# Decayed linear attention beside an FFN on one core: products and state of a token tile called in one piece

## The chip, the cores and the metric

One core of one Trainium2 chip runs the whole program. The metric is the device time of one execution in microseconds (us), and 854.63 us is the median of three runs. A profile of one further execution says what each engine did when: TensorE (PE, with its weight loads shown apart as PEld), VectorE (DVE), ScalarE (ACT), GpSimd (POOL) and SyncE (SP), which issues most transfers.

## The reference

Three stages follow each other. The first is a decayed linear attention with a bonus for the present token, over 4 sequences, 8 heads, 768 tokens and 48 numbers per head:

```python
for t in range(S):
    kt, vt, rt = (k[:, :, t], v[:, :, t], r[:, :, t])
    cur = np.einsum('bhd,bhe->bhde', u[None] * kt, vt)
    y[:, :, t] = np.einsum('bhd,bhde->bhe', rt, state + cur)
    state = w[None, :, :, None] * state + np.einsum('bhd,bhe->bhde', kt, vt)
```

The second is an FFN on all 3072 tokens of 384 numbers, with 2048 inner columns: `h = x @ w_in`, `g = h - tanh(h)`, `x = g @ w_out`. The third sends each token to the one of 8 experts that fits best (a normalised product with 8 embeddings), and puts it through that expert's two matrices (384 by 1024 and back) with a relu between, times the gate.

## The kernel before, in words

The 3072 tokens stand in 24 tiles of 128 (`n`), and three tiles make a block (`TB = 3`, eight blocks `j`). Tile `n` is chunk `n // 4` of sequence `n % 4`, so that the state a tile needs was left by the tile four places earlier.

Attention of one tile is an object `Att`. It is computed by chunk: `scores` (line 361) multiplies decayed keys `KT` with decayed queries `RT` into the PSUM tiles `pa`, two heads at a time on the two halves of the array; `causal` (line 366, DVE) copies the strictly causal part of `pa` over `am`, in which `diagonal` (line 350) had put the bonus of each token on the diagonal; `values` (line 391) multiplies `am` with the values and, for chunks after the first, `RT` with the old state, into the PSUM tile `py`, with outputs of 32 columns on the four quarters of the array side by side. `result` copies `py` into the block's operand `xt` as two halves, high and low, for the FFN (lines 396 and 397). `state` multiplies decayed keys with values (line 405, PSUM tile `pst`) and adds to the state (line 414). `values(part, of)` can run a part of its list of products. The list is ordered so that products with the old state come first.

The FFN takes one step `i` per 128 inner columns. `ffn1` (line 470) makes nine matmuls of 384 columns into a PSUM tile `ph`; `squares` and `small_tanh` turn it, on ACT and DVE, into `ghi` and `glo` (the last of these by line 533 on DVE); `ffn2` (line 481) makes nine matmuls into three accumulators, three steps later (`LAG = 3`).

In the main loop, from the block with `j = 0` on, an FFN step of block `j` is called, and then as many pieces of the attention of a later block as are due: `attn_tile` is a generator, a piece is what stands between two `yield`s, and a tile has six. Blocks 3 to 7 are due 18 pieces in 12 steps, so one and two pieces by turns, and a tile takes four steps. Block 2 is due 18 pieces in 8 steps. In each step `ffn1`, the pieces, then `ffn2` are called. The routing of the block before (`finish`) is also spread over the steps, and contains small DVE instructions such as line 610. At the first piece of a tile, the SP queue is given the two loads of the next one (`load_rkv`, lines 304 and 305).

The order of calls isn't yet the order on the engines. A planner goes through all instructions with a model of their times, takes those called earlier first, and takes later ones where the earlier aren't ready or have no buffer; what it makes is a fixed order for every engine. PSUM has eight tiles for all uses (`bufs=8`).

Of the kernel before, what the change touches and what calls it, by code (L numbers as in the profile page):

```python
# [29 lines left out]
def rwkv__then__tanh_ffn__then__top1_moe_kernel(  # L30
# [22 lines left out]
    HP = H // 2  # L53
# [372 lines left out]
    def attn_tile(n, xt):  # L426
        t = Att(n, xt)
        t.decay_r(nc.vector)
        t.decay_k(nc.gpsimd)
        t.bonus(nc.gpsimd)  # L430
        t.sums()
        t.diagonal()
        t.decayed()
        yield
        t.scores((0, 1))
        yield
        t.scores((2, 3))
        t.causal()
        yield
        t.values(0, 2)  # L440
        yield
        t.values(1, 2)
        t.result()
        yield
        t.state()
        yield

    xts = {}
# [8 lines left out]
    def attention(j):  # L457
        xts[j] = work.tile([P, NK, 2, TOK], F32R, name="xt")
        for n in range(TB * j, TB * j + TB):
            if 2 * TB + 1 < n + 1 < NTILE:  # L460
                load_rkv(n + 1)
            yield from attn_tile(n, xts[j])
# [915 lines left out]
```

## Time and profile before

| what | value |
|---|---|
| median of three runs | 854.63 us (853.89 to 856.8) |
| profiled execution | 856.98 us, of which 855.4 us are span from the first to the last instruction |
| PE busy | 791.2 us, 92% |
| DVE busy | 532.5 us, 62% |
| ACT busy | 442.9 us, 52% |
| POOL busy | 308.9 us, 36% |
| mean granted TensorE clock | 0.956 of full speed |

The page gives busy time by engine; the share of the span isn't the share of a stage. Matmuls overlap, so the start of one to the start of the next says more than the length of one. In the timeline, instructions of one kind that follow each other are merged (`x9`), with the start of the first and the time to the end of the last; what stands in brackets is idle time ahead of them and the engine that ended it.

### The profile page before, as it was taken

The numbers are of one execution on the slowest core, as the hardware profiler recorded it, in microseconds if no ns is written. First come the engines' busy times: TensorE is split into PE (matmuls) and PEld (weight loads), VectorE is DVE, ScalarE is ACT, GpSimd is POOL, SyncE is SP. The second block draws the span as 40 slices with busy tenths as digits, with TensorE's granted clock in tenths as the row PEclk, the third lists the DMA queues.
The fourth block names the chain that finished last, engine by engine and source line by source line (L and its number), as shares of the span: only waits on it lengthen the run. The fifth ranks groups of instructions, "written<-read, shape, count | busy, mean of one in ns | idle before, by whom it ended". The sixth has DMA issues, their size and how long they took to land. (4 is left out here: it accounts for less than half of the span.)

```text
span 855.4 us, 15321 instructions
## 1 busy us (share of the span) xinstructions
PE 791.2 (92%) x5835; PEld 726.7 (85%) x5835; DVE 532.5 (62%) x1048; ACT 442.9 (52%) x1007; POOL 308.9 (36%) x312
## 2 busy tenths in 40 slices
PE   6567969999999999999999999999979999999992
PEld 3456969888989989979989989999869999999992
DVE  8999697566775765665675574576553434544520
ACT  1156646645555656645745645778343434444421
POOL 6673352057461371353173070051243034321211
PEclk7579989999999999999999999999989999999996
DMA  8742612035213213213123021041354255545400
GB/s 292 266 147 65 242 56 75 1 82 160 82 53 109 81 54 108 81 53 108 42 93 109 20 63 57 29 117 60 102 187 128 75 168 167 166 141 171 128 27 29
DMA packets 41446, 89.69 MB, mean 105 GB/s; under 512 B 9328, under 2 KB 21024, under 8 KB 40338
## 3 DMA queue, kind: packets, MB, share of 16 engines
q1 hardware_dynamic: 37042, 79.10, 28.4%
q0 software_dynamic: 4320, 9.51, 3.5%
q8 instruction: 48, 0.79, 0.4%
q14 instruction: 36, 0.29, 0.1%
HBM read 69.82 MB, written 19.47 MB: 104 GB/s over the span
## 5 line engine op out<-in xcount | busy, mean ns | idle before, releaser
L470 PE MATMUL ph<-xt,wq 128*128 128x384 f32 (+2 forms) x1712 | 345.7, 344 | 3.0 <-DVE am L366 2.6
L470 PEld LDWEIGHTS ph<-xt,wq 128*128 128x128 f32 x1712 | 306.2, 191 | 9.1 <-DVE am L366 2.7
L481 PE MATMUL acc<-wq,ghi 128*128 128x392 f32 (+2 forms) x1120 | 296.5, 348 | 2.6 <-DVE wq L286 1.9
L481 PEld LDWEIGHTS acc<-wq,ghi 128*128 128x128 f32 (+1 forms) x1120 | 201.5, 188 | 14.0 <-issue 7.1
L481 PE MATMUL acc<-wq,glo 128*128 128x392 f32 (+2 forms) x560 | 187.6, 343 | 5.8 <-DVE glo L533 5.8
L517 ACT ACTIVATE z<-ph 128x384 f32<-128x384 f32 x128 | 62.4, 488 | 110.9 <-PE ph L470 110.6
L526 DVE TENSOR_TENSOR ph<-ph,z 128x384 f32<-128x384 f32 x128 | 71.9, 562 | 69.5 <-ACT z L517 69.1
L481 PEld LDWEIGHTS acc<-wq,glo 128*128 128x128 f32 (+1 forms) x560 | 104.9, 188 | 8.2 <-DVE glo L533 6.1
L533 DVE TENSOR_TENSOR glo<-ph,ghi 128x384 fp32r<-128x384 f32 x128 | 70.8, 553 | 35.8 <-ACT ghi L528 35.2
L528 ACT ACTIVATE ghi<-ph 128x384 fp32r<-128x384 f32 x128 | 62.6, 489 | 46.4 <-DVE ph L527 41.7
L702 POOL DMA_INDIRECT out_dram<-ob,gts x27 | 28.7, 1061 | 155.6 <-ACT ob L780 150.1
L518 ACT ACTIVATE q<-z,sb_t 128x384 f32<-128x384 f32 x128 | 78.9, 616 | 3.4
L527 DVE SCALAR_TENSOR_TENSOR ph<-q,ph 128x384 f32<-128x384 f32 x128 | 71.8, 561 | 13.6 <-ACT q L518 4.3
L547 DVE SCALAR_TENSOR_TENSOR glo<-ph,ghi 128x384 fp32r<-128x384 f32 (+2 forms) x56 | 31.5, 563 | 74.5 <-ACT ghi L546 63.5
L530 ACT ACTIVATE mk<-z,lz_t 128x384 bf16<-128x384 f32 x128 | 77.0, 602 | 0.0
L749 DVE TENSOR_TENSOR wq<-eraw,wq 128x768 fp32r<-128x768 f32 x60 | 55.4, 961 | 17.9 <-ACT wq L748 16.3
L546 ACT ACTIVATE ghi<-ph 128x384 fp32r<-128x384 f32 (+2 forms) x56 | 27.7, 496 | 72.7 <-PE ph L470 70.7
L748 ACT ACTIVATE wq<-eraw 128x768 fp32r<-128x768 f32 x64 | 50.5, 837 | 12.5 <-DMA eraw<-in_moe_w_dram 12.5
L335 POOL TENSOR_TENSOR rk<-rkv 128x384 f32<-128x384 f32 x21 | 22.0, 1049 | 92.4 <-DMA xs<-xr 88.8
L350 POOL TENSOR_TENSOR am<-ident,cd 128x512 f32<-128x512 f32 x42 | 45.0, 1094 | 14.4 <-DVE cd L340 14.4
L391 PE MATMUL py<-am,rkv 128*32 128x128 f32 x704 | 42.0, 295 | 7.7 <-DVE am L366 4.1
L327 POOL TENSOR_TENSOR tt<-tt,tab_k 112x512 f32<-112x512 f32 x20 | 36.7, 1835 | 29.5 <-DMA tt<-in_cols_dram 27.7
(272 smaller groups left out, 898.6 us busy)
## 6 DMA issues: line engine op xcount, KB each, us to landing
eraw<-in_moe_w_dram SPq DMA_DIRECT2D x32, 768.0 KB
rkv<-in_rows_dram SPq DMA_DIRECT2D x22, 640.0 KB
tt<-in_cols_dram SPq DMA_DIRECT2D x22, 448.0 KB
xd<-xt SPq DMA_DIRECT2D x8, 1152.0 KB
wraw<-in_moe_w_in_dram SPq DMA_DIRECT2D x8, 768.0 KB
wraw<-in_moe_w_out_dram SPq DMA_DIRECT2D x8, 768.0 KB
xs<-xr SPq DMA_DIRECT2D x21, 192.0 KB
first<-in_rows_dram SPq DMA_DIRECT2D x1, 640.0 KB
```

The costliest lines, as they stand in the source:

```text
L350: nc.gpsimd.tensor_tensor(out=a, in0=ident[:, None, :].to_broadcast([P, HP, P]), in1=self.cd[:, :, g:g + 1].to_broadcast([P, HP, P]), op=A ...
L470: nc.tensor.matmul(out=ph, lhsT=lhs[a][:, kk, :], rhs=rhs(b, kk), start=(kk == 0 and p == 0), stop=(kk == nk - 1 and p == 2))
L481: mm = nc.tensor.matmul(out=acc[t], lhsT=g[a][:, t * P:t * P + m], rhs=rhs(b, i), start=(i == span[0] and p == 0), stop=(i == span[1] - 1 ...
L517: nc.scalar.activation(out=z, in_=ph, func=AF.Square)
L518: nc.scalar.activation(out=q, in_=z, func=AF.Square, scale=SS, bias=sb_t)
L526: nc.vector.tensor_tensor(out=ph, in0=ph, in1=z, op=ALU.mult)
L527: nc.vector.scalar_tensor_tensor(out=ph, in0=q, scalar=KC, in1=ph, op0=ALU.add, op1=ALU.mult)
L528: nc.scalar.activation(out=ghi, in_=ph, func=AF.Copy)
L530: nc.scalar.activation(out=mk, in_=z, func=AF.Relu, bias=lz_t, accum_out=zx[:, step:step + 1])
L533: nc.vector.tensor_tensor(out=glo, in0=ph, in1=ghi.bitcast(F32), op=ALU.subtract)
L748: nc.scalar.activation(out=hi[c][:, a], in_=t[:, a], func=AF.Copy)
L749: engs[s % len(engs)].tensor_tensor(out=lo[c][:, a], in0=t[:, a], in1=hi[c][:, a].bitcast(F32), op=ALU.subtract)
```

## The change

`attn_tile` calls the same instructions in other pieces. Before, scores were called in two pieces, the products in two and the state in one. Now all scores and the causal copy are one piece, two pieces are empty, and all products, the state and the result are one piece, with the state's calls ahead of the result's. A tile still has six pieces.

```diff
@@ -432,17 +432,16 @@
         t.diagonal()
         t.decayed()
         yield
-        t.scores((0, 1))
-        yield
-        t.scores((2, 3))
+        t.scores(range(HP))
         t.causal()
         yield
-        t.values(0, 2)
         yield
-        t.values(1, 2)
+        yield
+
+        t.values()
+        t.state()
         t.result()
         yield
-        t.state()
         yield
```

## Rows read from the trace of the kernel before

**Rows 1.** The page, busy us, share and instructions of PE and others.

```profile
PE 791.2 (92%) x5835; PEld 726.7 (85%) x5835; DVE 532.5 (62%) x1048; ACT 442.9 (52%) x1007; POOL 308.9 (36%) x312
```

**Rows 2.** Windows: length, then busy us by engine, granted clock, DMA share, GB/s.

```profile
core 0: us, PE busy (x) PEld busy (x) DVE busy (x) ACT busy (x) POOL busy (x), PEclk, DMA share, GB/s
...
210.00:528.00 318.00, 313.07 (x2674) 283.02 (x2673) 206.82 (x433) 184.96 (x447) 124.68 (x123) 0.99 0.23 75
528.00:856.00 328.00, 305.73 (x1742) 297.09 (x1741) 154.44 (x335) 153.11 (x308) 79.02 (x75) 0.97 0.35 114
```

**Rows 3.** Groups of PE's matmuls by line, from 210 to 528 us.

```profile
L470 PE MATMUL ph<-xt,wq 128*128 128x384 f32 x684 | 132.5, 337 | 0.0
L481 PE MATMUL acc<-wq,ghi 128*128 128x392 f32 x460 | 127.9, 355 | 0.0
L481 PE MATMUL acc<-wq,glo 128*128 128x392 f32 x229 | 79.0, 345 | 0.0
L391 PE MATMUL py<-am,rkv 128*32 128x128 f32 x480 | 27.8, 280 | 4.4 <-issue 1.8 <-DVE am L366 1.3 <-DVE ph L527 1.2
L391 PE MATMUL py<-tt,st 112*32 112x128 f32 x360 | 27.7, 281 | 0.5 <-DVE glo L533 0.5
...
L590 PE MATMUL pk<-oh,ones 128*128 128x8 bf16 x30 | 1.6, 166 | 0.0
```

**Rows 4.** Timeline of PE, a step without attention: start us, us, instruction.

```profile
335.20 1.73 PE L470 MATMUL ph<-xt,wq 128*128 128x384 f32 x9
...
338.37 1.75 PE L470 MATMUL ph<-xt,wq 128*128 128x384 f32 x9
```

**Rows 5.** Timeline of PE, one tile: scores, first half, second half with state.

```profile
344.74 1.74 PE L470 MATMUL ph<-xt,wq 128*128 128x384 f32 x9
...
349.20 1.73 PE L470 MATMUL ph<-xt,wq 128*128 128x384 f32 x9
350.86 0.42 PE L391 MATMUL py<-tt,st 112*32 112x128 f32 x8
351.22 0.44 PE L481 MATMUL acc<-wq,ghi 128*128 128x392 f32 x1
...
353.71 1.75 PE L470 MATMUL ph<-xt,wq 128*128 128x384 f32 x9
355.39 0.30 PE L391 MATMUL py<-am,rkv 128*32 128x128 f32 x1
...
356.40 0.56 PE L405 MATMUL pst<-rkv,ktok 128*48 128x48 f32 x16
356.90 0.62 PE L481 MATMUL acc<-wq,ghi 128*128 128x392 f32 x2
```

**Rows 6.** Timeline of PE, a tile with its first half in three parts.

```profile
387.61 1.73 PE L470 MATMUL ph<-xt,wq 128*128 128x384 f32 x9
...
392.64 1.73 PE L470 MATMUL ph<-xt,wq 128*128 128x384 f32 x9
...
397.51 1.73 PE L470 MATMUL ph<-xt,wq 128*128 128x384 f32 x9
```

**Rows 7.** Timeline of PE, a tile whose first half is late.

```profile
366.62 1.81 PE L470 MATMUL ph<-xt,wq 128*128 128x384 f32 x9
...
370.98 0.41 PE L391 MATMUL py<-am,rkv 128*32 128x128 f32 x4 [1.25 <-DVE ph L527]
...
375.07 1.20 PE L470 MATMUL ph<-xt,wq 128*128 128x384 f32 x6
```

**Rows 8.** Timeline of DVE ahead of that half: a long instruction, the causal copies.

```profile
361.74 3.68 DVE L610 TENSOR_SCALAR rn<-rn 128x3 f32<-128x3 f32 x1
...
370.20 1.34 DVE L366 COPY_PREDICATED am<-cmask,pa 128x512 f32<-128x512 uint8 x2
```

**Rows 9.** Timeline, all engines: the next tile's columns are loaded, decayed, used.

```profile
309.03 0.34 SPq L304 DMA_DIRECT2D tt<-in_cols_dram  x1
...
313.13 1.80 POOL L327 TENSOR_TENSOR tt<-tt,tab_k 112x512 f32<-112x512 f32 x1 [1.59 <-DMA tt<-in_cols_dram]
...
316.14 1.16 PE L361 MATMUL pa<-tt 48*128 48x128 f32 x16
```

## The prediction

> **What bounds the kernel now.** I read the busy times first: TensorE (PE) is busy for 791.2 us, 92% of the span [rows 1]. Then the stretches: attention of the third to eighth token block runs beside the first FFN and ends at 528 us, and from 210 us (the start of the fourth block's) to there PE is busy for 313 of 318 us while VectorE (DVE) is busy for 207 and ScalarE (ACT) for 185; after 528 us, where no attention runs, PE is still busy for 306 of 328 us [rows 2]. So in the stretch that the change touches nothing but PE's own queue sets the pace, and what follows is PE work again, which starts earlier by what is saved here. The question is therefore how many PE microseconds each form of the attention costs.
>
> The timeline of PE answers that with a ruler. An FFN step is 9 matmuls of line 470 and 9 of line 481. Between two starts of line 470 a step without attention takes 338.37 - 335.20 = 3.17 us [rows 4], 0.176 us for a matmul. Whatever a step takes above that is attention. A tile of blocks 3 to 7 goes through four such steps (18 pieces in 12 steps): preparation, scores, first half of the products, second half with the state.
>
> - Scores: 349.20 - 344.74 = 4.46 us, so 1.29 us extra. They already run in one piece, both quarters in the same step.
> - First half: 353.71 - 349.20 = 4.51 us, 1.34 us extra, for 24 of the 56 matmul instructions of the products (480 + 360 over 15 tiles [rows 3]; each fp32 matmul is two instructions). The planner sent the 8 that read only the old state at 350.86, one FFN matmul at 351.22, the other 16 behind it [rows 5].
> - In five of the 15 tiles the half is cut into three: 392.64 - 387.61 = 5.03 us, 1.86 us extra [rows 6].
> - Second half with the state: 397.51 - 392.64 = 4.87 us, 1.70 us extra [rows 6]. Without the state (last chunk, 4 tiles) it is 0.50 us less, as the state's row takes 356.90 - 356.40 [rows 5]: 1.20 us.
> - The half that is late, in three of the 15 tiles: 375.07 - 366.62 = 8.45 us. PE stands still until 370.98, because the masked scores `am` aren't written [rows 7].
>
> **The change, part by part.** *What is removed.* In blocks 3 to 7 (15 tiles) the step of the first half becomes a plain step of 3.17 us. I take its cost today from the whole stretch, so that late ones count as they were: 684 + 460 + 229 = 1373 FFN matmuls in 318.0 us [rows 2, 3] at 0.1761 us are 241.8 us; 76.2 us are left. The routing's small matmuls take about 2.4 us of that (an estimate: 45 of them at the 1.6 us / 30 of the largest group [rows 3]). Scores: 15 x 1.29 = 19.4 us. Second halves: 11 x 1.70 + 4 x 1.20 = 23.5 us. That leaves 30.9 us for the first halves, 2.06 us each against 1.34 us for an undisturbed one; some 8 us of it are lateness like that of [rows 7], whose tile alone lost 8.45 - 4.51 = 3.9 us.
>
> *What is added.* The 24 instructions join the run of the second half. A run of 8 takes 351.22 - 350.86 = 0.36 us, a run of 32 takes 356.40 - 355.39 = 1.01 us [rows 5], so 24 more inside a run cost 0.65 us: 15 x 0.65 = 9.8 us. No instruction is added or dropped. What vanishes is the cost of entering and leaving: 0.36 us plus the slower matmul on either side, against 0.22 us for the same 8 inside a run.
>
> *Difference for blocks 3 to 7*: 30.9 - 9.8 = 21.1 us less on PE.
>
> *Block 2* (three tiles, before 210 us) has 18 pieces in 8 steps, and there the old and new products of the second and third tile are called in the same step; I count nothing for them. Its first tile had its first half a step early as above: 1.86 - 0.65 = 1.2 us, by the cut form.
>
> *The waits that move.* Products start one FFN step later than before, so `am` gets 3.17 us more. In the late tile `am` was complete at 370.20 + 1.34 = 371.54 us; the new run would start at 366.62 + 3.17 + 1.58 = 371.37 us, and its first 0.36 us needs no `am` [rows 7, 8]. So the lateness fits, with 0.2 us to spare. What was late there is DVE, held for 3.68 us by an instruction on 3 elements a partition [rows 8], one of three such holds, one ahead of each late half; the change doesn't move them. I take 0.5 us as not hidden in each of the three worst tiles: -1.5 us. Both ends for the range: nothing paid, or all 8 us paid as now.
>
> The Trainium skill, "SBUF — State Buffer", section "SBUF: two separate sides", says that DVE and GpSimd share one pair of ports as an exclusive lock, so that one of them can stand still for a whole instruction of the other. The trace shows the hold of 3.68 us [rows 8] and agrees with the rule, but doesn't name the holder. By that rule the hold would come back unchanged beside the same GpSimd work, and if PE paid it in full the sum would be the one of the lateness rival below.
>
> *State and result.* The state's matmuls are called before the result's copy, but PE already ran them right behind the products, and the copy waits for the products alone. The copy comes 0.65 us later in its step; the block's operand is read four FFN steps (12.7 us) later, which hides it. Two DVE additions of the state come before the result's subtraction, as they already did. No DMA is moved, but the SyncE queue loads the next tile's columns when the products end: issue at 309.03, decayed keys ready at 313.13 + 1.80 = 314.93, scores on PE at 316.14 [rows 9], 1.2 us spare. The products' end and the next scores both move by 0.65 us within that loop, so the spare time stays; if it were gone, PE would wait in order with all FFN matmuls behind it. PSUM: the products' bank is taken a step later, which frees one bank for that step; the new run needs no more banks at once than the old second half.
>
> *Sum*: 21.1 + 1.2 - 1.5 = 20.8 us. The profiled execution took 856.98 us, 855.4 of it span; 856.98 - 20.8 = 836.2. It stood 0.27% above the median of the runs, 854.63, so in terms of the median 836.2 x 854.63 / 856.98 = 833.9, say 834 us.
>
> **Rivals.**
> - *The planner cuts the run again.* The order on PE is worked out by a planner, and the first 8 instructions need only the old state. If in all 15 tiles two pieces are split off, each costs 0.36 + 0.20 - 0.22 = 0.34 us: 15 x 0.68 = 10.2 us back, 844 us. For it: it did so before. Against: it did so while `am` was missing; in the step of the second half, where all was there, it sent 32 and the state in one piece [rows 5]. 0.10.
> - *Lateness is paid elsewhere.* The 8 us aren't hidden but turn up before the new run or before line 481, which needs DVE's output: gain 20.8 - 6.5 = 14.3, 840 us. For it: only 0.2 us to spare in the late tile. Against: no FFN matmul of this stretch waits now except beside attention; its operands have three steps. 0.11.
> - *No gain at the end.* A fixed transfer or the planner's new order after 528 us gives it all back: 854.6 us. Against: PE busy 93% there [rows 2]. 0.05.
> - *Slower: the load loop becomes the bound.* Products end later in their step, so the next tile's columns do; if that load, then beside the block's store, came 3 us later than its slot, scores would wait 3.0 - 1.2 = 1.8 us in 17 tiles, 31 us, net +10: 865 us. It decides from 1.2 + 20.8 / 17 = 2.4 us of extra delay per tile. Against: the load took only 4.1 us from issue to use [rows 9]. 0.06.
> - My forecast, 834 us: 0.68.
>
> **How the numbers follow.** Bounds around the forecast: with no lateness paid and the second and third tiles of block 2 gaining about as much as two late ones (2 x 2.06 - 1.3 = 2.8 us), 25 us, 829.5 us; with lateness paid 840 us, with the run cut again 844 us. Range 829 to 844 us. 0.3% (2.6 us) is about what a measurement of this kernel can tell from no change. Faster by more: 0.68 + 0.10 + 0.11 = 0.89; same 0.05; slower 0.06.
>
> **What the profile after would show.** Right: every tile of blocks 3 to 7 has two visits to attention on PE, line 361 alone and line 391 followed by line 405; the step between them takes 3.17 us, the step of the run about 3.17 + 1.70 + 0.65 = 5.5 us; PE's waits for `am` in that stretch are nearly gone; counts of instructions are equal; the last product starts some 20 us earlier. Wrong: line 391 in more than one piece per tile; a wait of line 361 for GpSimd's decayed keys (the load loop); a wait of line 481 or 470 for DVE beside the 3.7 us hold; a later stage that stretches by what was saved. A granted clock below full speed in the longer run would also break the sum.

## The result, and the profile after

The changed kernel takes 833.6 us (median of 4 runs, 831.62 to 834.71) against 855.71 us before, measured beside it: a ratio of 0.9727, 95% interval 0.9674 to 0.978. The profiled execution took 832.75 us, 831.2 of it span, at a granted clock of 0.959. The forecast was 834 us, in a range of 829 to 844.

The page first: busy time of each engine, its share and its instructions.

```profile
PE 773.0 (93%) x5835; PEld 726.2 (87%) x5835; DVE 525.6 (63%) x1048; ACT 440.8 (53%) x1007; POOL 309.1 (37%) x312
```

Beside [rows 1] every count is equal: nothing was added or dropped, and PE is busy for 18.2 us less with the same 5835 instructions. The windows (length, busy us by engine, granted clock, DMA share, GB/s), cut where attention ends now:

```profile
core 0: us, PE busy (x) PEld busy (x) DVE busy (x) ACT busy (x) POOL busy (x), PEclk, DMA share, GB/s
...
210.00:506.00 296.00, 296.00 (x2670) 282.28 (x2669) 200.45 (x432) 182.47 (x446) 122.55 (x121) 1.00 0.24 76
506.00:832.00 326.00, 304.72 (x1742) 296.16 (x1740) 154.15 (x335) 152.58 (x307) 79.17 (x75) 0.97 0.36 115
```

[rows 2] needed 318 us for this work, with PE idle for 5 of them. It is done now in 296 us, and PE is never idle. The granted clock is 1.00, so the longer runs cost no clock. The groups of PE's matmuls in that window show which work got cheaper (busy us, mean ns, then idle time ahead):

```profile
L469 PE MATMUL ph<-xt,wq 128*128 128x384 f32 x684 | 132.3, 337 | 0.0
...
L391 PE MATMUL py<-am,rkv 128*32 128x128 f32 x480 | 22.5, 272 | 0.0
L391 PE MATMUL py<-tt,st 112*32 112x128 f32 x360 | 22.3, 276 | 0.0
```

The FFN's 684 matmuls cost what they cost in [rows 3]. The 840 of the products fall from 55.5 to 44.8 us, and the idle time ahead of them from 4.9 us to nothing. That idle time and what the busy columns lost are not the whole gain, because the records of neighbours overlap; the sum has to be made from starts. Here is PE in the tile that was late in [rows 7]:

```profile
354.74 1.74 PE L469 MATMUL ph<-xt,wq 128*128 128x384 f32 x9
...
356.40 1.16 PE L361 MATMUL pa<-tt 48*128 48x128 f32 x16
...
359.20 1.73 PE L469 MATMUL ph<-xt,wq 128*128 128x384 f32 x9
...
362.37 1.75 PE L469 MATMUL ph<-xt,wq 128*128 128x384 f32 x9
...
364.05 0.43 PE L391 MATMUL py<-tt,st 112*32 112x128 f32 x8
364.29 0.40 PE L391 MATMUL py<-am,rkv 128*32 128x128 f32 x8
...
365.72 0.56 PE L405 MATMUL pst<-rkv,ktok 128*48 128x48 f32 x16
...
367.91 1.75 PE L469 MATMUL ph<-xt,wq 128*128 128x384 f32 x9
```

Scores: 359.20 - 354.74 = 4.46 us, as in [rows 5]. The step of the former first half: 362.37 - 359.20 = 3.17 us, a plain step. The run: 367.91 - 362.37 = 5.54 us, products from 364.05 on and the state at 365.72 with no FFN matmul between. All 15 tiles of blocks 3 to 7 have one such run; without the state (four tiles) its step takes 5.03 to 5.05 us, and the first tile of a block has the routing's small matmuls in the step as well (5.80 us, or 5.30 without the state; 7.95 in block 3, where the step has 21 matmuls of line 480 in place of 9).

From the first plain step behind block 2 to the first plain step behind block 7, PE issues the same matmuls in both kernels: 1404 of the FFN, 840 of the products, 176 of the state, 240 of the scores. The starts of these steps, before and then after:

```profile
204.85 1.85 PE L470 MATMUL ph<-xt,wq 128*128 128x384 f32 x9
...
528.72 1.73 PE L470 MATMUL ph<-xt,wq 128*128 128x384 f32 x9
```

```profile
204.13 1.74 PE L469 MATMUL ph<-xt,wq 128*128 128x384 f32 x9
...
506.62 1.73 PE L469 MATMUL ph<-xt,wq 128*128 128x384 f32 x9
```

This took 528.72 - 204.85 = 323.87 us before and takes 506.62 - 204.13 = 302.49 us now: 21.4 us. Block 2 and all ahead of it gave 0.7 us, and what comes behind took 2.1 us less in this execution.

### The profile page after: what moved, and what is told of

Same layout as the page of the kernel before. It is cut to its first block, busy times and chain, and to the rows that moved or that the text cites. A ratio compares the mean times of both kernels' runs of the same rounds, so it can differ in the third digit from the quotient of the medians.

```text
span 831.2 us, 15313 instructions
## 1 busy us (share of the span) xinstructions
PE 773.0 (93%) x5835; PEld 726.2 (87%) x5835; DVE 525.6 (63%) x1048; ACT 440.8 (53%) x1007; POOL 309.1 (37%) x312
## 5 line engine op out<-in xcount | busy, mean ns | idle before, releaser
L480 PE MATMUL acc<-wq,ghi 128*128 128x392 f32 (+2 forms) x1120 | 291.2, 344 | 1.7 <-DVE wq L286 1.7
L254 POOL TENSOR_TENSOR wq<-wraw,wq 128x768 fp32r<-128x768 f32 x16 | 30.6, 1915 | 43.3 <-ACT wq L253 43.3
```

Source lines behind the costliest of these rows:

```text
L480: mm = nc.tensor.matmul(out=acc[t], lhsT=g[a][:, t * P:t * P + m], rhs=rhs(b, i), start=(i == span[0] and p == 0), stop=(i == span[1] - 1 ...
```

## The experiments

Eight kernels, in two groups, each beside the kernel before on its own chip (858.63 us for those labelled x, 858.15 us for those labelled y):

| run | what it is | median us | ratio to before, 95% |
|---|---|---|---|
| x1 | after, the 8 instructions on the old state a step earlier | 852.07 | 0.9927 (0.9892 to 0.9962) |
| x2 | after, the whole run a step earlier | 857.77 | 1.0000 (0.9975 to 1.0025) |
| x3 | before, scores in one call | 858.43 | 1.0011 (0.9985 to 1.0036) |
| x5 | before, two small instructions moved off DVE | 852.63 | 0.9933 (0.9911 to 0.9955) |
| y0 | after, unchanged | 835.25 | 0.9729 (0.9699 to 0.9759) |
| y1 | x1 with the two instructions moved off DVE | 842.13 | 0.9809 (0.9781 to 0.9837) |
| y2 | x2 with the two instructions moved off DVE | 859.37 | 1.0010 (0.9986 to 1.0034) |
| y3 | after, nine steps for block 2 in place of eight | 834.80 | 0.9722 (0.9691 to 0.9752) |

Line numbers in their rows differ by one or two from those of after. A visit is a stretch of attention's products on PE with FFN matmuls on either side. The theory: a visit costs something to enter and leave, whatever is done in it, so fewer visits are the gain, and lateness is hidden by the later call. The rivals: the gain is the later call alone (lateness), or it is the scores' call, or something else in the order. The state's call ahead of the result's was not tried alone; PE ran the state's matmuls right behind the products before the change too [rows 5].

**x3: the scores' call alone.**

```diff
-        t.scores((0, 1))
-        yield
-        t.scores((2, 3))
+        t.scores(range(HP))
         t.causal()
         yield
+        yield
```

> The kernel before, with only the scores called in one piece and the causal copy a piece earlier. PE's order has the scores in one piece already, so no change against before by both theories (855 us, within 0.3%). If the scores' part of the edit had a share in the gain, it would show here, by as much as it is faster.

1.0011: no effect. This part of the diff is worth nothing, since the scores already ran in one piece.

**x1: one visit more per tile.**

```diff
+        t.values(0, 7)
         yield
 
-        t.values()
+        for i in range(1, 7):
+            t.values(i, 7)
         t.state()
```

> The kernel after, but the first turn of the products (8 of the 56 matmul instructions of a tile, those that need the old state and no masked scores) is called one FFN step earlier, where the first half stood before. In PE's order this is one visit more in each of the 15 tiles of blocks 3 to 7, and nothing in it can be late. If a visit has a price of its own (0.36 us for the 8 instructions and 0.20 us on the matmuls beside them, less 0.22 us for the same 8 inside a run), 15 x 0.34 = 5.1 us and a little more in block 2: 839 us against 833.6. If all of the gain came from the masked scores being ready in time, and visits cost nothing by themselves, no change: 833.6 us.

852.07 us, where after would be 858.63 x 0.9729 = 835.4 us on this chip: 16.7 us are lost. Two things happened. The visit has its price: where nothing is late, the early step takes 3.74 us and the run 5.33, against 3.16 and 5.54 before the split, some 0.37 us for a tile and 5.5 us for fifteen. The other 11 us are a cost of another kind, about half of it in blocks 3 to 7 and half in block 2 (44.95 us there against 39.90). PE around one such early visit in x1 (the bracket is idle time and what ended it):

```profile
368.70 1.80 PE L471 MATMUL ph<-xt,wq 128*128 128x384 f32 x9 [0.52 <-DVE row L598]
371.77 0.42 PE L391 MATMUL py<-tt,st 112*32 112x128 f32 x8 [1.27 <-DVE glo L534]
```

and DVE ahead of it:

```profile
364.17 4.23 DVE L611 TENSOR_SCALAR rn<-rn 128x3 f32<-128x3 f32 x1
...
371.16 0.56 DVE L534 TENSOR_TENSOR glo<-ph,ghi 128x384 fp32r<-128x384 f32 x1 [0.27 <-ACT ghi L529]
```

The 8 instructions need only the old state, which is long there, and yet PE stands still for 1.27 us until line 534 is done. That line reads `ph`, and `py` and `ph` come from the same pool of eight PSUM buffers with one tag. So the visit needs no late operand, but it needs a buffer, and a late DVE still has them; the wait for line 534 is measured, that it is for the buffer is read from the code. DVE is late by the long hold at 364.17. So an early visit doesn't only cost its entry; it is one more place where lateness can be paid.

**x5: the holds alone, in the kernel before.** The instruction held in [rows 8] and one like it go to GpSimd.

```diff
-        nc.vector.tensor_tensor(out=pos, in0=pos, in1=oh, op=ALU.mult)
+        nc.gpsimd.tensor_tensor(out=pos, in0=pos, in1=oh, op=ALU.mult)
...
-        nc.vector.tensor_scalar(out=rn, in0=rn, scalar1=1e-6, scalar2=None, op0=ALU.add)
+        nc.gpsimd.tensor_scalar(out=rn, in0=rn, scalar1=1e-6, scalar2=None, op0=ALU.add)
```

> The kernel before, with two small instructions of the routing (the 1e-6 added to the norm, 3 elements a partition, and a product of 24 elements) moved from DVE to GpSimd; these are the ones that took 3.7 us on DVE ahead of the late first halves. PE's order stays nearly that of before, with all its visits. If the holds on DVE are what made those halves late, three steps fall from 8.5, 6.4 and 6.5 us to 4.5 to 5.0 us: 7 to 8 us faster than before, 848 us. If the halves were late for another reason (a PSUM bank, the causal copy itself), no change: 855 us.

852.63 us, 6 us less than before. The late half of [rows 7] in x5:

```profile
370.43 1.73 PE L470 MATMUL ph<-xt,wq 128*128 128x384 f32 x9
372.09 0.43 PE L391 MATMUL py<-tt,st 112*32 112x128 f32 x8
...
374.93 1.75 PE L470 MATMUL ph<-xt,wq 128*128 128x384 f32 x9
```

Its step takes 374.93 - 370.43 = 4.50 us in place of 8.45, and the other two late steps fall from 6.40 and 6.51 to 4.50 and 4.51. Blocks 3 to 7 take 316.2 us (323.87 before): the holds cost them 7.7 us, which fits the "some 8 us" of the prediction. The edit leaves 34 visits in the first halves (two in eleven tiles, three in four). The run gained less than 7.7 us since block 2's third tile lost 4.2 us: there DVE waits in its queue for a load (4.83 us at line 324, at 202.34), with the causal copies behind it, and PE stands still for 3.23 us.

**y1: the extra visit without the holds.** The diffs of x1 and x5 together.

> The first turn of the products a step early, and the two small routing instructions moved to GpSimd as in the run without holds. PE's order is that of the run with the first turn early. If that run lost its 18 us against after to the price of a visit alone, it stays as slow (0.993 of before). If it lost 0.36 us a tile to the visit and the rest to the 4.2 us holds of DVE, this one has the visits' price only in blocks 3 to 7: 15 x 0.36 = 5.4 us over after there, and some 5 us in block 2: 0.985 of before.

842.13 us. The price of the visit can now be read clean. One tile of y1:

```profile
343.38 1.73 PE L471 MATMUL ph<-xt,wq 128*128 128x384 f32 x9
345.04 0.43 PE L391 MATMUL py<-tt,st 112*32 112x128 f32 x8
345.40 0.62 PE L482 MATMUL acc<-wq,ghi 128*128 128x392 f32 x2
...
347.12 1.75 PE L471 MATMUL ph<-xt,wq 128*128 128x384 f32 x9
```

347.12 - 343.38 = 3.74 us against 3.17, so 0.57 us for 8 instructions alone; the run gets 0.21 us shorter for it. 0.57 - 0.21 = 0.36 us a tile is the price of a visit. Blocks 3 to 7 take 308.6 us against 302.7 in y0: 5.9 us, 0.39 a tile, and no wait of PE is left there. The whole list of PE's waits between 205 and 530 us, in x1 and then in y1 (waited for, us in total, times, longest):

```profile
engine line waited for: us in total, times, longest us
PE py L391 <- DVE glo L534: 3.5, 4, 1.3
PE ph L471 <- DVE cntb L601: 0.9, 1, 0.9
PE ph L471 <- DVE row L598: 0.5, 1, 0.5
```

```profile
core 0 of [0], span 839.2 us
engine line waited for: us in total, times, longest us
```

The second list is empty: with the holds gone, the buffer is free in time, and about 10 us of x1 (852.07 - 842.13) were lateness, about half of it in block 2 (44.95 us there in x1, 39.45 in y1). The 5 us that the expectation left for block 2 didn't come. Of the other 842.13 - 835.25 = 6.9 us the visits are 5.9; the rest stands behind attention, where executions differ by some 2 us.

**x2 and y2: the whole run a step earlier**, with the holds (x2) and, by the two lines of x5, without (y2).

```diff
         yield
-        yield
-
         t.values()
         t.state()
         t.result()
         yield
+        yield
         yield
```

> The kernel after, with its one run of products, state and result called one FFN step earlier. The planner finds the masked scores not ready there and cuts the run: 8 instructions, one FFN matmul, the other 48 and the state (two of three tiles). If the two parts of the gain are both real, this has one visit more a tile than after, 15 x 0.34 = 5 us, and the lateness back where a hold of DVE falls ahead of it, up to 8 us: 839 to 847 us. If calling the products together were all, 834 us; if calling them late were all, near 855 us.

> The one run of products, state and result a step early, and the two small routing instructions on GpSimd. If that run's lateness came from holds of DVE, it falls to after plus one visit a tile, 5 us, and what block 2 loses: 0.985 of before. If it came from calling the products before the masked scores can be there at all, it stays within 0.5% of the run early with holds (1.000 of before).

857.77 and 859.37 us: the whole gain is lost in both, and the 839 to 847 us of x2's first expectation was missed. PE of y2 at one second tile of a block:

```profile
318.15 1.83 PE L468 MATMUL ph<-xt,wq 128*128 128x384 f32 x9
...
320.99 0.43 PE L391 MATMUL py<-tt,st 112*32 112x128 f32 x8 [1.01 <-DVE glo L531]
...
322.76 0.41 PE L391 MATMUL py<-am,rkv 128*32 128x128 f32 x4 [0.97 <-DVE am L366]
...
326.85 1.73 PE L468 MATMUL ph<-xt,wq 128*128 128x384 f32 x9
```

and DVE there:

```profile
319.92 0.55 DVE L340 TENSOR_REDUCE cd<-rk 128x8 f32<-128x384 f32 x1 [0.68 <-POOL rk L336]
...
321.99 1.33 DVE L366 COPY_PREDICATED am<-cmask,pa 128x512 f32<-128x512 uint8 x2
```

No long hold is in sight here, and the run still stands on `am`: the causal copies end at 321.99 + 1.33 = 323.32 us, and the products are due just before 320. They hang on line 340, which waits for GpSimd's line 336, and on GpSimd's line 350 behind it (2.04 us from 320.55 on): in the order that GpSimd has here, that chain ends too late for this place. The step takes 8.70 us, where one with the same pieces and no wait takes 5.87 (x2, at 353.30). PE's waits in y2 between 205 and 530 us:

```profile
PE py L391 <- DVE am L366: 5.0, 10, 1.0
PE pk L583 <- DVE oh L580: 4.4, 4, 1.5
PE py L391 <- DVE glo L531: 2.7, 3, 1.0
```

Blocks 3 to 7 take 322.5 us in y2 with one FFN step less among them than in y0; with that step it would be 322.5 + 3.17 = 325.6 us, 23 more than in y0. 12.1 of them are these waits and some 4.7 the twelve visits that y2 has more; the rest isn't taken apart. Only 5.0 us are waits for `am`, and in x2 it is 1.1 of 9.4. Nor are all holds gone in y2: line 574, another small instruction of the routing, takes 2.05 us at 359.37 beside GpSimd, and PE's 4.4 us of waiting for `oh` come behind such instructions. So taking the two instructions off DVE doesn't bring the gain back at this place; that `am` comes too late there is one part of the loss and not all of it.

**y0 and y3: after again, and block 2 in nine steps.**

```diff
-    NATT0 = 8
+    NATT0 = 9
```

> The kernel after, unchanged, beside the three others of this call, so that they are compared on one chip. 0.973 of before, as measured.

> The kernel after, with block 2's 18 pieces of attention spread over 9 FFN steps and not 8 (NATT0 = 9), so that a tile takes three steps and its products come two steps after its scores. The third tile's products come out in one visit in PE's order, the second's in two. From the steps of after, block 2 costs 14.8 us above plain FFN and three clean tiles 3 x 3.65 = 11 us: 3 to 4 us faster than after, 830 us. If the first FFN's own waits fill what is freed, no change.

y0 repeats the gain on the chip of its group: 0.9729. Its blocks 3 to 7 take 302.7 us (302.49), its part behind them 326.4 us, as long as the 326.7 us of before. So the 2.1 us that this part gave in the profiled execution of after differ from one execution to the next; I take none of them as the change's. y3 is not measurably better (834.80 against 835.25), and the 3 to 4 us expected didn't come: its third tile of block 2 now runs in one piece in a step of 5.59 us, but its second tile takes 8.22 us with a wait of PE for `am` of 1.49 us. No version tried beats the changed kernel.

## Why the prediction was right

**The ruler and the price of a run: right.** The plain step stays at 3.17 us. The run was put at 3.17 + 1.70 + 0.65 = 5.52 us and takes 5.54; without the state at 3.17 + 1.20 + 0.65 = 5.02, and takes 5.03. 24 matmul instructions inside a run cost 0.65 us, as the rows said that were compared (8 against 32).

**What vanishes is the visit: shown.** The prediction priced a split-off piece at 0.34 us; y1 measured 0.36 to 0.39. The Trainium skill, "TensorEngine Tiling (Array Packing)", section "Key Properties", says that a change of tiling mode drains TensorE. The FFN's matmuls are 128*128 and the products' 128*32 and 112*32, and the trace agrees with a cost of entering and leaving; it shows neither a drain as such nor what a change of shape inside a run costs.

**The sum for blocks 3 to 7: 21.1 us forecast ahead of lateness, 21.4 measured.** The experiments take it apart. From before to x5 (the holds ahead of the late halves gone, pieces as they were but for one tile) 323.9 - 316.2 = 7.7 us, the lateness. From x5 to after 316.2 - 302.5 = 13.7 us, the merging, 0.91 us a tile. It takes 34 visits away, so 0.40 us each, close to the 0.36 to 0.39 of y1 for a single one. By the prediction's rows an undisturbed first half costs 1.34 us in ten tiles and 1.86 in five, 22.7 us in all; less the 9.8 us that its instructions cost in the run that is 12.9.

**Lateness that doesn't return: right in the outcome, wrong in the reason.** That the late half stood on `am` is right: [rows 7] name line 527, but that ended at 370.29, and the first of the two causal copies (0.73 us from 370.20 on) at 370.93, just ahead of PE's 370.98. The step that failed is "the change doesn't move them", said of the three long holds of DVE, and with it the -1.5 us. In the profiled execution they are short at those places (1.24, 1.24 and 1.34 us). DVE's held instruction, and GpSimd around it, in after at the tile of [rows 8]:

```profile
355.67 1.24 DVE L609 TENSOR_SCALAR rn<-rn 128x3 f32<-128x3 f32 x1
```

```profile
353.16 2.04 POOL L350 TENSOR_TENSOR am<-ident,cd 128x512 f32<-128x512 f32 x2
355.16 1.73 POOL L327 TENSOR_TENSOR tt<-tt,tab_k 112x512 f32<-112x512 f32 x1
357.82 1.05 POOL L601 DMA_INDIRECT tab<-tokid,irow  x1 [0.93 <-DVE irow L598]
```

In the kernel before, line 327 came ahead of line 350 here and GpSimd ran without a pause from 360.62 to 366.36 us; the changed calls made the planner put line 350 first, and GpSimd pauses after line 327, where the hold ends: 1.24 us in place of 3.68. One long hold is left in blocks 3 to 7, in the second tile of block 3, and it tests the slack. DVE and GpSimd there, from after:

```profile
229.78 3.93 DVE L616 TENSOR_SCALAR se<-se 128x3 f32<-128x3 f32 x1
...
238.36 0.74 DVE L366 COPY_PREDICATED am<-cmask,pa 128x512 f32<-128x512 uint8 x1
```

```profile
229.01 1.79 POOL L327 TENSOR_TENSOR tt<-tt,tab_k 112x512 f32<-112x512 f32 x1 [1.82 <-DMA tt<-in_cols_dram]
230.76 1.01 POOL L335 TENSOR_TENSOR rk<-rkv 128x384 f32<-128x384 f32 x1
231.73 1.01 POOL L331 TENSOR_TENSOR ktok<-rkv,ktab 128x384 f32<-128x384 f32 x1
232.70 1.00 POOL L336 TENSOR_TENSOR rk<-rk,u_bc 128x384 f32<-128x384 f32 x1
```

`am` is complete at 238.36 + 0.74 = 239.10 us, and PE's first product with it starts at 239.97: 0.87 us to spare behind a hold of 3.93 us, and the step takes its 5.54 us. In y0, the same kernel, the hold at that place is short, and one comes back at the third of the old places:

```profile
478.25 3.17 DVE L609 TENSOR_SCALAR rn<-rn 128x3 f32<-128x3 f32 x1
...
485.23 1.36 DVE L366 COPY_PREDICATED am<-cmask,pa 128x512 f32<-128x512 uint8 x2
```

`am` is complete at 486.59 us there, PE's first product with it starts at 486.89, 0.30 us later, and PE doesn't wait. So even holds that came back were covered, as the prediction had said ("0.2 us to spare"); the 0.5 us a tile that it paid all the same was not due. In 9 of the 15 tiles of after `am` has less than 3.17 us to spare (0.87 to 2.96), so a run called one step earlier finds it missing there, unless the order changes too. Which part of the gain the new order of GpSimd has by itself was not tried in the changed kernel.

**Block 2: 1.2 us forecast, 0.6 measured** (40.54 us before, 39.90 now; 39.73 in y0). The first tile gave what was said: its run takes 5.54 us and the step ahead is plain. The second and third tile, counted at nothing, lost some 0.6 us: the third's scores are cut in two and its run too, the second's products are cut in three with the state in a visit of its own, and PE waits 1.30 us for the second's `am`.

**The rivals.** Cut again: every tile of blocks 3 to 7 has one run, so no. Lateness paid elsewhere: PE has no wait at all from 205 to 530 us. No gain at the end: the part behind attention takes what it took (326.4 us in y0 against 326.7). The load loop: PE stands still nowhere ahead of line 361 in blocks 3 to 7. The counts, the plain step, the run's step and the clock, which the prediction named as its marks, all came as said. The sum made against the profiled execution was 20.8 us; between the profiled executions it was 856.98 - 832.75 = 24.2 us: 3.4 more, of which 0.3 come from blocks 3 to 7, 1.5 from lateness that wasn't paid, 2.1 from the part that varies between executions, less 0.5 for block 2. That the median of 833.6 us stands so close to 834 is in part luck: between medians the gain is 855.71 - 833.6 = 22.1 us against 854.63 - 833.9 = 20.7 forecast, and before stood 1.1 us higher in the median of four than in that of three.

## What to carry to other kernels

Where one engine's queue sets the pace, price small work by the step it sits in (start to start), alone and inside a run: here a piece costs 0.36 to 0.39 us more as a visit of its own, and 15 tiles with a visit less, and without its cuts, were 13.7 us. Merging paid only where the last operand of the whole run was ready: called one step earlier, the run was cut again and had to wait, and the merging was worth nothing. A piece that waits for no operand may still wait for a buffer, so "early because its inputs are there" isn't free either.

## What the runs showed of the hardware that was not expected

A DVE instruction on 3 elements a partition was held for 3.7 to 4.2 us (3.68 before, 3.93 after, 4.23 in x1), over four GpSimd instructions and not one. Each of these holds ends within 0.04 us of the end of a GpSimd instruction: 229.78 + 3.93 = 233.71 against 232.70 + 1.00 = 233.70 us, and the short one too, 355.67 + 1.24 = 356.91 against 355.16 + 1.73 = 356.89. The Trainium skill, "SBUF — State Buffer", section "SBUF: two separate sides", has the two share one pair of ports as a lock, held for a whole instruction. The trace agrees with GpSimd as the holder, and a hold here lasted over as many as four of its instructions. GpSimd's order alone doesn't set the length. Here is the instruction that was held for 3.93 us in after, now in y0, where GpSimd runs lines 327, 335, 331 and 336 in the same order:

```profile
229.14 1.05 DVE L616 TENSOR_SCALAR se<-se 128x3 f32<-128x3 f32 x1
```

```profile
228.37 1.79 POOL L327 TENSOR_TENSOR tt<-tt,tab_k 112x512 f32<-112x512 f32 x1 [2.07 <-DMA tt<-in_cols_dram]
230.13 1.02 POOL L335 TENSOR_TENSOR rk<-rkv 128x384 f32<-128x384 f32 x1
```

It was done at 230.19 us, at the end of the first, though the next followed at once. What decides between one and four is open. Where GpSimd paused, as after line 327 in after, the hold ended there: 1.24 us.
